# Casts moved off GpSimd, gated weight loads, a table of ranks for 239 tasks, and x block stores in another order

## The chip, the cores and the metric

One core of a Trainium2 chip. The time is the device time of one execution in microseconds (us). A profile's "span" is about 1.7 us shorter than the device time of the same execution. Repeats were taken on five chips, called A to E here, always with the kernel before on the same chip.

## The reference, cut to what matters

```python
q_p, k_p = phi(q), phi(k)                 # phi(x) = max(x, exp(x) - 1 if x <= 0) + 1, 8 x 8 heads, 576 x 64
kv  = einsum('bhsd,bhse->bhde', k_p, v);  z = k_p.sum(2)
att = (q_p @ kv) / (q_p . z)              # -> x, 4608 tokens x 512
P   = exp(x @ w_gate); 8 rounds of row and column normalisation     # 4608 x 8
out = sum_e P[:, e:e+1] * (relu(x @ w1[e]) @ w2[e])                 # 8 experts, 512 -> 1024 -> 512
```

## The kernel before: the parts that the change and the argument touch

The program is a list of tasks with durations, priorities and buffer pools. A small planner places each task on its engine in simulated time; the result is a fixed order for each engine. Attention comes in 16 blocks (numbers 0 to 15), each with one k, q and v input of 576 KB. Expert 0 is computed beside them ("hq" is its first layer, "ye" its second). From about 190 us on, units of the other experts (the sparse part) fill TensorE almost without a gap.

```python
# inputs of block n: blocks 2 and 3 go through GpSimd's queue, behind the first w1 load, the rest through SyncE's
(nc.gpsimd if n in (2, 3) else nc.sync).dma_start(out=..., in_=...)
...
tvv.append(fadd(("pool", 1.3), f_v, deps=[ta, tin["v"]], ...))      # v cast fp32 -> fp16 on GpSimd
vcast[n] = tvv[0]
...
w_t = {0: load_w1(0, prio=-290.0, parts=2, deps=[vcast[0]])}        # weight loads are issued by GpSimd
if b == 1:
    w_t[0] += load_w2(0, prio=-96.5, parts=2, deps=[in_prev[0]])    # w2 of expert 0: behind block 3's inputs
...
w_t[1] = load_w1(1, prio=0.0, after=110.0) + load_w2(1, prio=0.0, after=115.0)
```

The exponential of a k or q block ("ek", "eq") runs on ScalarE. The copy that empties a bank of ye ("acc") runs on ScalarE or VectorE. And each engine works strictly in its order.

The softmax here doesn't subtract the row's maximum and nothing guards it: scores larger than these inputs give would overflow.

## Time and profile before

| | us |
|---|---|
| device time, median of 3 (range) | 982.42 (981.93 to 982.49) |
| the same on chips A to E, medians of 9 to 11 runs | 981.85, 981.97, 981.72, 981.88, 981.87 |
| TensorE busy in the profile | 962.2 of 982.2 |
| device time of the profiled execution | 983.97 |

The profiled execution is 1.5 us slower than the median. And the kernel before has a spread of its own: of its 53 repeats on the five chips, 42 lie at 980.6 to 982.6 and 11 at 983.5 to 985.4.

The view of waits sums, by line, the idle time of an engine and what ended it. For TensorE of the kernel before, from 22.5 to 120 us, the four largest of its ten lines (columns: line, releaser, us in total, times, longest):

```profile
PE hq L536 <- ACT h L540: 2.2, 3, 1.4
PE qt_ps L332 <- DVE tq L281: 1.6, 1, 1.6
PE ye L706 <- DVE acc L223: 0.9, 1, 0.9
PE num_ps L371 <- DVE xn L376: 0.9, 3, 0.4
```

In all ten lines the releaser is VectorE or ScalarE. No line names a DMA: before the change no transfer holds TensorE up directly from 22.5 us on.

### The profile page before, as it was taken

How to read it: one execution, taken by the hardware profiler on the slowest of the kernel's cores; microseconds unless marked ns; L12 is line 12 of the kernel's file. 1: busy time of each engine (PE TensorE's matmuls, PEld its weight loads, DVE VectorE, ACT ScalarE, POOL GpSimd, SP SyncE). 2: the span in 40 equal slices, each digit the busy share in tenths (PEclk: the TensorE clock that was granted, in tenths of full speed). 3: DMA queues.
4: the chain of work that ended last, by engine and by line, in shares of the span. 5: the costliest groups of instructions: out<-in, count | busy, mean ns of one | idle time of the engine just before them, and what ended most of it. 6: DMA issues, size and time to landing. Idle time of an engine off the chain costs nothing.

```text
span 982.2 us, 21403 instructions
## 1 busy us (share of the span) xinstructions
PE 962.2 (98%) x8716; PEld 792.7 (81%) x8716; DVE 771.7 (79%) x1561; ACT 563.2 (57%) x1034; POOL 127.9 (13%) x171
## 2 busy tenths in 40 slices
PE   7899999999999999999999999999999999999997
PEld 4455564488888888888888888888888888888885
DVE  6898869967777777777777777777777777777774
ACT  4798754565555555555555555555555555555552
POOL 4111200001111111111111111111111111111110
PEclk9999999999999999999999999999999999999999
DMA  9886953162226312272225322272225322236663
GB/s 318 257 303 239 265 160 140 65 127 77 75 76 142 97 73 76 76 161 76 77 75 137 101 76 75 76 162 76 76 76 137 102 76 76 76 103 168 161 161 98
DMA packets 47029, 121.99 MB, mean 124 GB/s; under 512 B 4177, under 2 KB 18001, under 8 KB 46929
## 3 DMA queue, kind: packets, MB, share of 16 engines
q1 hardware_dynamic: 32128, 99.76, 30.3%
q0 software_dynamic: 14480, 20.33, 11.5%
q8 instruction: 68, 1.11, 0.5%
q10 hardware_dynamic: 320, 0.52, 0.1%
q14 instruction: 33, 0.26, 0.1%
HBM read 119.69 MB, written 17.69 MB: 140 GB/s over the span
## 4 chain that ended last, share of the span: by engine, by line
PE 89%; DVE 1%; ACT 1%; issue 0%
PE ye L809 33%; PE hq L627 23%; PE att L627 11%; PE Zye L627 6%; PE Zye L809 6%; PE ye L706 5%; PE hq L536 4%; PE xt_ps L387 0%; PE kv_ps L306 0%; PE num_ps L371 0%; PE lg_ps L405 0%; DVE tk L281 0%; PE qt_ps L332 0%; ACT tq L272 0%; PE den_ps L347 0%; ACT qpT L221 0%
## 5 line engine op out<-in xcount | busy, mean ns | idle before, releaser
L823 DVE SCALAR_TENSOR_TENSOR acc<-ye,P_sb,acc 128x256 f32<-128x256 f32 x620 | 264.9, 477 | 95.3 <-PE ye L809 77.9
L627 PEld LDWEIGHTS <-W 128*128 128x128 f16 x2016 | 197.1, 98 | 23.7
L809 PEld LDWEIGHTS <-S 128*128 128x128 f16 x1984 | 194.1, 98 | 22.7 <-issue 0.3
L809 PE MATMUL ye<-T,S 128*128 128x256 f16 x1488 | 192.8, 273 | 0.1
L833 POOL TENSOR_TENSOR acc<-acc,st 128x256 f32<-128x256 f32 x124 | 87.5, 725 | 625.6 <-ACT st L830 620.7
L653 ACT ACTIVATE h<-hq 128x512 f16<-128x512 f32 x126 | 76.3, 606 | 160.8 <-PE hq L627 160.8
L627 PEld LDWEIGHTS <-w 128*128 128x128 f16 x1512 | 147.6, 98 | 23.3 <-issue 1.0
L809 PEld LDWEIGHTS <-h 128*128 128x128 f16 x1488 | 145.6, 98 | 16.8
L627 PE MATMUL hq<-xs,W 128*128 128x256 f16 x1008 | 151.2, 273 | 0.0
L627 PE MATMUL att<-xs,W 128*128 128x256 f16 x1008 | 151.2, 272 | 0.0
L627 PE MATMUL hq<-xs,w 128*128 128x256 f16 x1008 | 140.7, 272 | 0.8 <-DVE h L656 0.8
L782 DVE TENSOR_TENSOR S<-h 128x1024 f16<-128x1024 f16 x124 | 85.4, 688 | 57.9 <-ACT h L653 57.9
L656 DVE CUSTOM_DVE_ANT_0 h<-att,s 128x512 f16<-128x512 f32 x126 | 86.7, 688 | 13.1 <-ACT s L643 13.1
L830 ACT ACTIVATE st<-Zye,P_sb 128x256 f32<-128x256 f32 x124 | 52.1, 471 | 78.0 <-PE Zye L809 78.0
L643 ACT COPY s<-hq 128x512 f32<-128x512 f32 x126 | 75.0, 595 | 36.7 <-PE hq L627 36.7
L650 ACT ACTIVATE h<-Zye 128x512 f16<-128x512 f32 x126 | 75.2, 597 | 35.1 <-PE Zye L627 35.1
L656 DVE CUSTOM_DVE_ANT_0 h<-hq,s 128x512 f16<-128x512 f32 x126 | 86.5, 686 | 0.8 <-PE hq L627 0.7
L639 ACT COPY Zye<-hq 128x512 f32<-128x512 f32 x126 | 73.3, 581 | 16.3 <-PE hq L627 16.3
L706 PE MATMUL ye<-w,h 128*128 128x512 f16 x320 | 77.6, 379 | 0.9 <-DVE acc L223 0.9
L627 PE MATMUL Zye<-xs,w 128*128 128x256 f16 x504 | 75.6, 273 | 0.0
L647 ACT COPY s<-att 128x512 f32<-128x512 f32 x126 | 74.5, 591 | 0.0
L536 PE MATMUL hq<-xT,w 128*128 128x512 f16 x288 | 70.6, 379 | 2.4 <-ACT h L540 2.2
(90 smaller groups left out, 963.1 us busy)
## 6 DMA issues: line engine op xcount, KB each, us to landing
xs<-xd SPq DMA_DIRECT2D x63, 896.0 KB, 4.6
w<-in_moe_w_dram POOLq DMA_DIRECT2D x14, 1024.0 KB, 11.7
out_dram<-acc SPq DMA_DIRECT2D x68, 128.0 KB, 2.4
kin<-in_k_dram SPq DMA_DIRECT2D x14, 576.0 KB, 6.0
qin<-in_q_dram SPq DMA_DIRECT2D x14, 576.0 KB, 5.0
vin<-in_v_dram SPq DMA_DIRECT2D x14, 576.0 KB, 6.4
xd<-xst SPq DMA_DIRECT2D x9, 512.0 KB, 2.6
xd<-xT SPq DMA_DIRECT2D x9, 256.0 KB, 7.1
```

The lines of the kernel that those rows point to most:

```text
L536: nc.tensor.matmul(ghq["tile"], lhsT=gw1["tile"][:, c, ts(f, P)], rhs=xT[:, c, ds(512 * g, 512)], start=(c == 0), stop=(c == NDT - 1))
L627: nc.tensor.matmul(dst[:, p, :], lhsT=lhs(p, c), rhs=rhs(c), start=(first and p == 0 and c == 0), stop=(c == 1), skip_group_check=True)
L643: nc.scalar.copy(out=gs2["tile"], in_=gX["tile"])
L647: nc.scalar.copy(out=gs5["tile"], in_=gR["tile"])
L650: nc.scalar.activation(out=hd(0, 0), in_=Zt[1], func=AF.Relu)
L653: nc.scalar.activation(out=hd(1, 0), in_=gX["tile"], func=AF.Relu)
L656: nc.vector._custom_dve(TENSOR_ADD_SAT, out=dst, in0=ps, in1=sb, s0=3.0e38, s1=0.0)
L706: nc.tensor.matmul(gy[tt]["tile"], lhsT=gh["tile"][:, f, ds(P * tt, P)], rhs=gw2["tile"][:, f, :], start=(f == 0), stop=(f == NFT - 1))
L782: nc.vector.tensor_tensor(out=Sx[:, i], in0=a0, in1=a1, op=op)
L809: nc.tensor.matmul(bank(g_)[:, s, :], lhsT=lhs(s, kk), rhs=rhs(kk), start=(new and s == 0 and kk == 0), stop=(kk == 3), skip_group_check=True)
L823: nc.vector.scalar_tensor_tensor(out=dst(), in0=bank(g_)[:, s, :], scalar=P_sb[:, gg, e:e + 1], in1=dst(), op0=ALU.mult, op1=ALU.add)
L833: nc.gpsimd.tensor_tensor(out=dst(), in0=dst(), in1=gst["tile"], op=ALU.add)
```

## The change

The intent: take the 16 v casts off GpSimd, where they slow VectorE down; issue weight loads when v has landed instead of when its cast is done (a "gate", a copy of four columns); pin 239 tasks to ranks, and 50 of them to one engine too; and put the raw x copies behind the sums. The diff, cut to its core:

```diff
-    p_e = S_.pool(2)
+    p_e = S_.pool(3)                                  # a third buffer of exponentials
-        tvv.append(fadd(("pool", 1.3), f_v, deps=[ta, tin["v"]],
+        tvv.append(fadd(("act", 1.17) if n < 2 else ("dve", 0.75), f_v, deps=[ta, tin["v"]],
-        vcast[n] = tvv[0]
+        if n in (0, 13, 15):
+            def f_gate(_):
+                nc.gpsimd.tensor_copy(out=gate, in_=gin["v"]["tile"][:, 0, 0, 0:4])
+            gates[n] = add(("pool", 0.15), f_gate, deps=[tin["v"]], use=[gin["v"]], prio=pr)
-    w_t = {0: load_w1(0, prio=-290.0, parts=2, deps=[vcast[0]])}
+    w_t = {0: load_w1(0, prio=-290.0, parts=2, deps=[gates[0]])}
+        if g == 0:                                    # the first two hq run in halves
+            jobs = [(f, c, c + 2) for c in (0, 2) for f in range(2)] + jobs[2:]
-        ti = add(("sp", 0.2), f_raw, deps=deps + [t_close], prio=0.0)
+        ti = add(("sp", 0.9), f_raw, deps=deps + [t_close, ti], prio=0.0)   # after the store of the sums
-    w_t[1] = load_w1(1, prio=0.0, after=110.0) + load_w2(1, prio=0.0, after=115.0)
+    w_t[1] = load_w1(1, prio=0.0, deps=[gates[13]]) + load_w2(1, prio=0.0, deps=[gates[15]])
+    ranks = """ 43:-88.9997 46:-94.9994:act 55:-94.9991:dve ... """       # 239 entries, cut here
+    for w in ranks.split():
+        n, p, *en = w.split(":")
+        t = S_.t[int(n)]
+        t["prio"] = float(p)
+        if en:
+            t["eng"] = {en[0]: t["eng"][en[0]]}
```

## The prediction

> **What bounds the kernel now.** I read the page first (busy time by engine and by slice), then the table of windows, then the timelines of TensorE, VectorE and GpSimd in the first 150 us, then the chain of waits.
>
> The table of windows, cut where the behaviour changes (columns: window, length, busy us of PE, weight loads, VectorE, ScalarE and GpSimd with instruction counts, granted clock, DMA share, GB/s):
> ```profile
> 0.00:22.50 22.50, 17.05 (x148) 9.15 (x149) 15.77 (x34) 9.51 (x14) 11.06 (x19) 0.92 0.99 311
> 22.50:120.00 97.50, 88.84 (x963) 53.94 (x961) 85.54 (x178) 83.07 (x132) 19.08 (x16) 1.00 0.85 270
> 120.00:150.00 30.00, 30.00 (x339) 18.38 (x337) 21.21 (x55) 15.51 (x31) 0.00 (x0) 1.00 0.67 183
> 150.00:220.00 70.00, 70.00 (x424) 41.36 (x423) 58.20 (x147) 38.18 (x68) 3.06 (x4) 1.00 0.37 102
> 220.00:975.00 755.00, 754.14 (x6845) 669.04 (x6843) 589.48 (x1147) 416.92 (x792) 94.69 (x132) 1.00 0.35 99
> ```
> From 120 us to 975 us TensorE is never free (at most 0.9 us in 855), at full clock. The chain of waits says the same: 89% of the span is PE. The change touches the attention part, the first expert's first layer and the x block stores, all before about 200 us. So it can only win what TensorE loses in the first 120 us, and the first question is how much that is.
>
> The timeline of TensorE around its first stalls (start, us, engine, what, and in brackets the idle time before it and who ended it):
> ```profile
> 22.53 0.99 PE L536 MATMUL hq<-xT,w 128*128 128x512 f16 x3
> 23.68 1.24 PE L536 MATMUL hq<-xT,w 128*128 128x512 f16 x5 [0.16 <-ACT xT L221]
> 26.29 1.02 PE L536 MATMUL hq<-xT,w 128*128 128x512 f16 x4 [1.36 <-ACT h L540]
> 29.49 0.68 PE L332 MATMUL qt_ps<-ident,tq 128*128 128x128 f16 x9 [1.55 <-DVE tq L281]
> 44.63 1.02 PE L706 MATMUL ye<-w,h 128*128 128x512 f16 x4 [0.95 <-DVE acc L223]
> ```
> The reader sees two regimes. Before 22.53 us TensorE has only the first two attention blocks and 34 filler matmuls on a zero tile. Read from start to start, a 128x512 matmul in a run takes 0.2155 us, and one attention block takes 2.62 us (18 kv 0.63, 9 qt 0.53, 10 den 0.30, 10 num 0.56, 10 xt 0.60). So of 22.53 us, 2 x 2.62 = 5.2 are useful and **17.3 are lost**. After 22.53 us the stalls that the timeline lists up to 120 us are 0.16, 1.36, 1.55, 0.17, 0.95, 0.40, 0.29, 0.77, 0.54, 0.55, 0.27, 0.24, 0.30 and 0.86: **8.4 us**. As a check, counting the work up to 150 us (359 wide matmuls x 0.2155 = 77.4, 16 blocks x 2.62 = 41.9, logits and others 4.4) gives 123.7, so 26.3 are lost, 17.3 + 9.0.
>
> Why those stalls are there shows in the timeline of all engines:
> ```profile
> 6.60 1.43 DVE L281 SCALAR_TENSOR_TENSOR tk<-kin,ek 128x576 f16<-128x576 f32 x2
> 12.39 1.15 POOL L225 CAST vv<-vin 128x1152 f16<-128x1152 f32 x1 [0.28 <-DMA vin<-in_v_dram]
> 12.41 2.40 DVE L281 SCALAR_TENSOR_TENSOR tk<-kin,ek 128x576 f16<-128x576 f32 x2
> 27.06 2.37 DVE L281 SCALAR_TENSOR_TENSOR tq<-qin,eq 128x576 f16<-128x576 f32 x2
> 27.25 1.58 POOL L225 CAST vv<-vin 128x1152 f16<-128x1152 f32 x1 [3.15 <-DMA vin<-in_v_dram]
> ```
> The same pair of VectorE instructions takes 1.43 us alone and 2.37 to 2.40 beside a GpSimd cast. The tq at 27.06 is the one that TensorE waits 1.55 us for at 29.49. The third such case (tk from 41.60, 2.38 us, beside the cast at 41.70) is directly ahead of the acc copy that ends the 0.95 us stall at 44.63.
>
> **What the Trainium skill says.** "SBUF — State Buffer", section "Who interferes with whom": VectorE with two SBUF inputs contends with a GpSimd instruction that reads SBUF, through a port pair the two share. The trace agrees: +0.95 us on a pair, and the cast itself 1.58 instead of 1.15. "VectorE: DVE Perf Modes", section "The perf-mode tier table": a copy from fp32 in SBUF runs at two elements a cycle. No instruction of that form is in the trace, so the cost of the new VectorE cast is an estimate: the fp16 minimum over 1152 elements takes 0.45 us here, at four a cycle and the page's 0.96 GHz 0.30 of that is elements and 0.15 fixed, hence 0.60 + 0.15 = 0.75 us. "Perfetto Trace Analysis", section "Identifying the Most-Contended Engine": matmul busy time is a poor measure since matmuls overlap. The trace agrees (a wide matmul is listed with 379 ns on average and costs 215), so I count start to start.
>
> **The change part by part.**
> (1) *No cast on GpSimd.* Removed: 16 casts x 1.238 = 19.8 us of an engine that is idle anyway. Removed with them: the collisions, from the group means against the clean times tk 22 x (0.923 - 0.715) = 4.6, tq 16 x (0.814 - 0.715) = 1.6, ek 16 x (0.550 - 0.450) = 1.6, eq 16 x (0.496 - 0.450) = 0.7, together 8.5 us of VectorE. Added: 14 x 0.75 = 10.5 us on VectorE, 2 x 1.17 = 2.3 on ScalarE (taken as its exp on the same shape, 1.166). Pinned ranks move other work: up to the last xT copy VectorE does 1 acc copy for 6, 24 kvz copies for 30 and 14 xT copies for 16; ScalarE 19, 40 and 18 for 10, 34 and 16. Counts by group means: VectorE 121.9 to 118.1 us, ScalarE 112.3 to 122.8 (parts of neighbours overlap, so true occupancy is lower). Neither fills the 137 us that this stretch takes.
> (2) *Gated weight load.* The first load is issued when a 4-column copy ends, not a 1.15 us cast: about 8.0 us for 9.00. DMA is saturated from there to 40 us (share 1.09 to 1.14 in ten-microsecond windows), so what follows lands about 1 us earlier.
> (3) *Order at the start.* I walked the new order by hand with durations of the trace. The first blocks' tq is made by ScalarE add plus VectorE maximum, the second block's tk comes uncollided at 13.0 (14.8 before), its xn ends at 21.4 (22.1), xT at 22.8 (23.6). Two hq matmuls run ahead of the last transposes; 16 are done by 26.1, with one wait of about 1 us for the relu to free a bank; the v cast of the third block ends at 27.2 and its kv matmuls at 27.8. Before, the same work (16 hq, kv, qt) was done at 30.9: 3.1 ahead. At 33.0 the new order has 32 hq and two blocks' kv done; before had 28 hq at 35.46, and needs 0.86 more: **3.3 us** gained.
> (4) *Stalls after 42 us*: 5.2 of the 8.4. Those behind VectorE lateness should shrink, but the new order is just as fixed, and a few late results must be expected. I take 2.2 as left: **3.0 us** gained.
> (5) *Stores.* Before, the raw copies went out at 104 to 139 us, now each follows its own sums, from about 140 to 180. The x tile's memory is reused from 195 us, when the last hq of the first expert is read. The sums end at 179.8, a transfer lands in 7 us: 187, hidden. **0.**
> Sum: 982.4 - 3.3 - 3.0 = **976.1**.
>
> **Rivals.** *The start is bound by DMA*: third and fourth v landed at 22.95 and 27.25, and reordering does not move bytes. Then part 3 gives 1 and the total is 978.5. For it: share above 1.0. Against it: 1.36 and 1.55 us of stalls there are ended by ScalarE and VectorE. *ScalarE becomes the bound*: 10.5 us more on it, and every hq bank waits for its relu. New waits of hq on h would eat parts 3 and 4: 981 to 984. Against it: it is idle 13 of the first 22.5 us. *The ranks fit the chip well*: almost all stalls vanish, 17.3 - 1 and about 1 left: 973. *The late stores hold up the x tile's release or the first xs load*: some us lost near 195 to 210; I see 8 us of slack.
>
> **Range and chances.** All that can be won is about 8.4 to 9 plus 1 to 1.5 at the start, so 972 is the floor, and 2% (962.8) is out of reach. Repeats lie within 0.6 us. The ScalarE rival alone sets the upper end, at half its effect: range 972.8 to 980.2. Faster by over 2%: 1%, within 2%: 98%, slower: 1%.
>
> **What would show it.** Right: no VectorE tk or tq pair above 1.6 us; v casts of 0.75 on VectorE; first hq near 21 and ye near 33; stalls after 22 us summing to 3 or 4; the windows from 220 us unchanged. Wrong: hq waiting on h again and again (ScalarE), waits on DMA at kv, idle TensorE between 180 and 215 (stores), or casts of 1.3 us on VectorE.

## The result, and the profile after

| | median us | runs |
|---|---|---|
| after | 980.35 | 977.64, 980.62, 981.61, 980.07 |
| before, same chip | 982.17 | 981.43 to 982.49 (4 runs) |

The ratio is 0.9979, 95% interval 0.9957 to 1.0001. A ratio is the mean time of one kernel's fast runs over that of the other's fast runs of the same rounds, so not quite the ratio of the medians. The class is "same", as predicted, but 980.35 lies just outside the range. The runs are as telling as the median: 4 us apart, where the prediction reckoned with 0.6.

The profiled run after is the fastest of the four (977.64). Its table of windows, the answer to the one of before:

```profile
0.00:22.50 22.50, 16.98 (x153) 9.31 (x154) 14.47 (x36) 14.08 (x18) 9.32 (x18) 1.00 0.98 311
22.50:120.00 97.50, 93.71 (x985) 55.85 (x984) 84.52 (x179) 89.18 (x152) 2.00 (x4) 1.00 0.84 259
150.00:220.00 70.00, 70.00 (x452) 44.06 (x451) 62.15 (x156) 37.38 (x67) 7.27 (x6) 1.00 0.61 175
```

TensorE is busy 93.71 of the 97.5 us in the front against 88.84 before. GpSimd falls from 19.08 to 2.00 us, and between 150 and 220 us TensorE is never idle, as before. The timeline of TensorE:

```profile
20.48 0.59 PE L545 MATMUL hq<-xT,w 128*128 128x512 f16 x2
25.84 0.68 PE L335 MATMUL qt_ps<-ident,tq 128*128 128x128 f16 x9 [0.33 <-DVE tq L281]
32.68 1.03 PE L718 MATMUL ye<-w,h 128*128 128x512 f16 x4
36.98 1.02 PE L718 MATMUL ye<-w,h 128*128 128x512 f16 x4 [1.36 <-DMA w<-in_moe_w_dram]
108.66 1.02 PE L718 MATMUL ye<-w,h 128*128 128x512 f16 x4 [0.52 <-ACT acc L221]
```

The first hq comes at 20.48 us (22.53 before), the first ye at 32.68 (35.58), and the wait for tq is 0.33 (1.55). Then come two waits that the kernel before does not have: **1.36 us for a weight tile** and **0.52 us for a bank copy**. On VectorE (timeline) the pair beside which a cast used to run is back at its clean time, and the new cast costs what was estimated:

```profile
11.31 1.43 DVE L281 SCALAR_TENSOR_TENSOR tk<-kin,ek 128x576 f16<-128x576 f32 x2
24.36 1.43 DVE L281 SCALAR_TENSOR_TENSOR tq<-qin,eq 128x576 f16<-128x576 f32 x2
25.70 0.76 DVE L223 CAST vv<-vin 128x1152 f16<-128x1152 f32 x1
```

The chain that ended last shows where the two new waits come from. In order of time (start, us, what) it now holds, after one q input at the start, two transfers:

```profile
17.95 18.99 DMA w<-in_moe_w_dram
97.76 9.05 DMA kin<-in_k_dram
```

The first is the second half of expert 0's w2. It is issued when it always was (17.2 us for the pair, 17.5 before), but takes 19.0 us to land. The view of transfers has the two halves together, with the median from issue to landing; first the kernel before, then the changed one:

```profile
w<-in_moe_w_dram POOLq DMA_DIRECT2D x2, 512.0 KB, 13.8
```
```profile
w<-in_moe_w_dram POOLq DMA_DIRECT2D x2, 512.0 KB, 16.5
```

SyncE now issues block 4's k at 24.02 instead of 26.72, since the buffers come free earlier, and ye asks for the tile 2.9 us earlier. The second is the last k input (block 15). One microsecond behind its issue, at 98.91, GpSimd issues the second expert's w1 (1 MB as it lands; the 2 MB in some expectations counts it as read, in fp32), released by the gate on block 13's v; before, that load left at 112.35, behind all inputs. On ScalarE's timeline the k input is what the next three steps hang on:

```profile
106.83 1.16 ACT L266 ACTIVATE ek<-kin 128x1152 f16<-128x1152 f32 x1 [0.77 <-DMA kin<-in_k_dram]
108.02 0.58 ACT L221 COPY acc<-ye 128x512 f32<-128x512 f32 x1
```

The exponential waits for k, the bank copy stands behind the exponential, and TensorE waits for the bank (0.52 us at 108.66).

### The profile page after: what moved, and what is told of

Same layout as the page of the kernel before. It is cut to its first block, busy times and chain, and to the rows that moved or that the text cites. A ratio compares the mean times of both kernels' runs of the same rounds, so it can differ in the third digit from the quotient of the medians.

```text
span 975.9 us, 21395 instructions
## 1 busy us (share of the span) xinstructions
PE 960.9 (98%) x8716; PEld 791.7 (81%) x8716; DVE 767.9 (79%) x1562; ACT 568.9 (58%) x1049; POOL 111.9 (11%) x158
## 4 chain that ended last, share of the span: by engine, by line
PE 91%; DMA 3%; ACT 3%; DVE 1%; issue 1%; POOL 0%; SPq 0%; DVEq 0%; ACTq 0%; POOLq 0%
PE ye L821 33%; PE hq L639 23%; PE att L639 11%; PE ye L718 6%; PE Zye L639 6%; PE Zye L821 6%; PE hq L545 4%; DMA w<-in_moe_w_dram 2%; DMA kin<-in_k_dram 1%; ACT eq L266 1%; PE xt_ps L390 1%; ACT h L549 1%; DMA qin<-in_q_dram 1%; PE num_ps L374 0%; ACT tq L272 0%
## 5 line engine op out<-in xcount | busy, mean ns | idle before, releaser
L821 PEld LDWEIGHTS <-S 128*128 128x128 f16 x1984 | 194.1, 98 | 22.5
L651 ACT COPY Zye<-hq 128x512 f32<-128x512 f32 x126 | 73.2, 581 | 17.5 <-PE hq L639 17.5
```

The costliest lines, as they stand in the source:

```text
L821: nc.tensor.matmul(bank(g_)[:, s, :], lhsT=lhs(s, kk), rhs=rhs(kk), start=(new and s == 0 and kk == 0), stop=(kk == 3), skip_group_check=True)
```

## The experiments

The theory: the order of the changed kernel has little slack, so two transfers that share the DMA engines with others (w2 at 37 us, the last k at 107 us) turn into waits, of a length that varies from run to run. The main rivals: the granted clock of the run makes the spread; the late stores cost; the ranks or the casts do not bring what was reckoned.

### The changed kernel again, three times (chip A)

No edit.

> The changed kernel itself, five rounds. Four runs so far gave 977.64 to 981.61, the kernel before 981.43 to 982.49. Theory D (the front now hangs on DMA landings: the w2 half load took 19.0 us in the one trace and a kin load 9.05 us, both on the chain of waits): the spread of 3 to 4 us comes back, with every span 974 to 980 and the kernel before again within 1 us. Theory C (the clock gate: some runs have TensorE at half clock for a few us in the front): the spread comes back too, but the slow runs are those with the lower mean clock (0.995 against 1.0), in order. Theory N (it was noise of one chip): spread under 1.5 us, median near 977 or near 981.

> A second trace of the changed kernel. Theory D: if this execution is slower than 977.6, TensorE's stalls that are longer than in the first trace (1.8 us of lost time at 36.98 behind w2) are behind a DMA landing, and the windows from 220 us on are the same. Theory C: the window table shows a granted clock under 1.00 in the front and the matmuls there at 427 ns start to start.

> A third trace of the changed kernel, same expectations as the second: theory D a longer stall behind w2 or an input load, theory C a window with clock under 1.00 after 20 us.

Measured: again 979.42 median (976.46 to 979.90, and one run of 985.61), ratio 0.9978 (0.9952 to 1.0003). The two looks gave 981.68 and 976.93. Their traces differ mainly in the two waits and the clock after one of them. The slower one, timeline of ScalarE and TensorE:

```profile
109.07 1.16 ACT L266 ACTIVATE ek<-kin 128x1152 f16<-128x1152 f32 x1 [2.71 <-DMA kin<-in_k_dram]
110.90 1.36 PE L718 MATMUL ye<-w,h 128*128 128x512 f16 x4 [2.65 <-ACT acc L221]
```

and its windows (columns as above; the third number from the end is the granted clock):

```profile
110.00:112.00 2.00, 1.10 (x4) 0.44 (x4) 0.00 (x0) 1.98 (x4) 0.00 (x0) 0.86 1.05 355
112.00:114.00 2.00, 2.00 (x13) 1.40 (x12) 0.74 (x2) 1.52 (x3) 0.00 (x0) 0.50 0.38 149
114.00:116.00 2.00, 2.00 (x35) 1.06 (x34) 1.74 (x3) 0.93 (x4) 1.22 (x2) 0.78 0.00 0
```

After a stall of 2.65 us the clock falls to half for some microseconds, which costs another 2 x (0.14 + 0.50 + 0.22) = 1.7 us. In the faster look the same exponential starts at 105.94 without a wait, and w2 holds TensorE up for 0.65 us. The mean clock of a run does not order the runs: both looks have 0.998, since the faster one's dip lies at 8 to 14 us and costs little there: its first hq comes at 21.00 us, against 20.62 in the slower look. So the clock follows a stall here and lengthens it; it is not what starts the spread.

### The stores alone undone (chip A)

```diff
-        ti = add(("sp", 0.9), f_raw, deps=deps + [t_close, ti], prio=0.0)
+        ti = add(("sp", 0.9), f_raw, deps=deps + [t_close], prio=0.0)
```

> One part undone: the raw x copies no longer wait for the sums in issue order. My working: 0 us, equal to the changed kernel within its spread (976 to 981). If the stores' order was worth something (rival): 2 us or more either way, and the windows between 140 and 220 us show idle TensorE in the slower of the two.

Measured: 980.92 (977.69 to 981.18), ratio 0.9978, as the changed kernel beside it. Inconclusive at this size: its profile has the part from the first sparse unit to the end at 788.2 us (979.0 - 190.79) against 787.0 (975.9 - 188.86), with some 0.7 us of TensorE's idle time at 190 to 220 us, but that is one trace. The edit is also not the stores alone: the planner put 76 of VectorE's and 18 of TensorE's instructions in other places, from about 145 us on, so the stores' own worth stays unsettled.

### One cause away at a time (chip B)

The second expert's w1 issued with its w2; nothing else in any engine's order moves (the traces have the same order of instructions, apart from this issue):

```diff
+                if e == 1 and nm == "w1":       # held, and issued ahead of the next weight load
+                    held.append(go)
+                    return
```

> The changed kernel with one issue moved: the second expert's w1 load (2 MB) leaves right ahead of its w2 load, at about 114 us, in place of 98.9 us; the order of every instruction on TensorE, VectorE, ScalarE and SyncE is that of the changed kernel. Theory (the early load shares the DMA engines with the last k block, whose exponential stands ahead of a bank copy on ScalarE): the k load of the last block lands 6 to 7.5 us after its issue in place of 8.0 to 11.2, ScalarE does not wait for it, TensorE has no stall over 0.4 us between 104 and 112 us, the granted clock does not dip there, and the fast runs lie at 975.5 to 977.5 within 2 us of each other. Rival (the spread has another cause, the clock of the chip or the rest of the kernel): the stall goes but the fast runs still spread over 3 us, with a median of 979 to 980.5. Second rival (the weights now come too late): TensorE waits for w1 of the second expert after 120 us, and the time is 980 or more.

Block 4's inputs through GpSimd's queue, so behind w2; the orders of TensorE, VectorE and ScalarE stay, as the traces show:

```diff
-                (nc.gpsimd if n in (2, 3) else nc.sync).dma_start(
+                (nc.gpsimd if n in (2, 3, 4) else nc.sync).dma_start(
```

> The changed kernel with the inputs of block 4 issued from GpSimd's queue behind the first expert's w2 load in place of SyncE's, so that the second half of w2 shares the DMA engines with less; all other orders stay. Theory: the second half of w2, 18.99 us from issue to landing in the changed kernel, takes 17 us or less, the 1.36 us stall of TensorE at 37 us falls under 0.5, and the time falls by 0.8 to 1.3 us; the run-to-run spread of 3 us stays, as the early w1 load is still there: median 978 to 979.5. Rival (the transfer is bound by bytes and not by who is ahead): the wait moves to block 4's own inputs, and the time stays at 979 to 980.5.

> Both edits of the two runs beside it. Theory: the two gains add: no stall over 0.5 us at 37 us nor between 104 and 112 us, fast runs at 974.5 to 976.5 within 2 us of each other, 0.6 to 0.8 per cent under the kernel before and clear of it. Rival (one of them has another cause): no better than the better of the two alone, 977 or more, or a spread of 3 us.

The early w1 put into the kernel before. This edit is not as clean: from 107 us on the planner gave ScalarE, VectorE and TensorE another order, so it shows a new plan with an early w1:

```diff
-    w_t[1] = load_w1(1, prio=0.0, after=110.0) + load_w2(1, prio=0.0, after=115.0)
+    w_t[1] = load_w1(1, prio=0.0, deps=[vcast[13]]) + load_w2(1, prio=0.0, after=115.0)
```

> The kernel before with one line of the change alone: the second expert's w1 load held only to the v cast of block 13, not behind all inputs. Theory (the early load delays the last k block and hurts a schedule whose ScalarE has little slack there): the last k block lands 8 us or more after its issue in place of 6.2 to 7.3, and TensorE's stalls between 100 and 115 us grow by 0.5 to 2.5 us: 982.5 to 984.5, with a wider spread. Rival (only the tighter order of the changed kernel has no slack): the k block lands later, but the time stays within 0.5 us of the kernel before, 981.5 to 982.5.

| chip B | median us | runs | ratio (95%) |
|---|---|---|---|
| w1 held | 979.00 | 977.92 to 982.10 | 0.9967 (0.9949 to 0.9984) |
| block 4 behind w2 | 975.87 | 975.71 to 975.92, and one of 977.83 | 0.9935 (0.9919 to 0.9950) |
| both | 975.80 | 975.56 to 976.26 | 0.9931 (0.9916 to 0.9945) |
| before with early w1 | 981.42 | 981.21 to 981.88 | 0.9988 (0.9972 to 1.0005) |

The two halves of w2 land in 12.7 us (block 4 behind w2) and 13.8 us (both edits) in the median, near the 13.8 of the kernel before, and in 17.8 with w1 held alone. The view of transfers with block 4 behind w2:

```profile
w<-in_moe_w_dram POOLq DMA_DIRECT2D x2, 512.0 KB, 12.7
```

This landing varies by itself, too: in the kernel before with early w1, whose order is that of the kernel before up to that time, the median is 15.4.

Three of my expectations missed. With w1 held the wait at 108 us was gone, as expected, but the spread was not: in its profile the wait for w2 is 2.66 us, and the clock falls behind it (0.95 and 0.71 in the two five-microsecond windows from 35 us). And block 4's inputs behind w2 came out 3.1 us under w1 held alone, and 3.5 to 4.5 under the changed kernel's medians on other chips (it did not run on chip B), where 0.8 to 1.3 was expected, with little spread; that left open whether the early w1 mattered at all, or whether chip B was kind. The kernel before with early w1 loses nothing (981.42 against 981.97), where 0.5 to 2.5 us were expected, although its last k then takes 12.3 us to land: the exponential of that k starts only 13.7 us after the issue (112.72 against 99.04), so it does not wait. In the kernel before it starts 7.4 us after the issue (108.72 against 101.28), which 12.3 would have held up. So it is the new order that hides the landing, and what the early w1 alone would cost is not shown. The view of transfers, issue to landing of that one k input, for the kernel before with early w1:

```profile
kin<-in_k_dram SPq DMA_DIRECT2D x1, 576.0 KB, 12.3
```

### The parts of the change by themselves (chip C)

> The changed kernel itself once more, on the chip of the three runs beside it (it was not among those of the earlier set with block 4 on GpSimd's queue). Theory (its loss is two waits on DMA landings, for the second half of the first expert's w2 at 37 us and for the last k block at 107 us, each of a length that changes from run to run): fast runs between 976.4 and 982 and more than 2 us apart, with a median 2 to 4 us over the 975.9 of block 4 on GpSimd's queue. Rival (that result belongs to its chip): this kernel lies at 976 to 977 here as well, all runs within 1 us.

> Block 4's inputs on GpSimd's queue, the table of ranks kept, and the v casts back on GpSimd (the ranks were searched without them, and five engine choices of ScalarE casts fall out). Theory (casts on GpSimd cost through slowed VectorE instructions, 1.3 us of lateness each where they meet): VectorE's pair instructions that run beside a cast take up to 1.4 us in place of 0.75, and the time is 978.5 to 981, 2.6 to 5 us over the same kernel with the casts on VectorE. Rival (the ranks are the gain, and the cast is worth nothing by itself): within 1 us of 975.9.

> Block 4's inputs on GpSimd's queue and the casts off GpSimd, but without the table of ranks, so that the plan's own order stands. Theory (the table is what brings hq, kv and ye forward; its removal costs what the prediction gave it and more): first hq later than 21.5 us, more TensorE stalls between 22 and 120 us (5 us or more in all), and 978.5 to 981.5. Rival (the table adds little once the casts are gone): 975.5 to 977.

> Block 4's inputs on GpSimd's queue, casts on GpSimd and no ranks: what is left of the change are the third buffer of exponentials, the split first hq, the gates and the order of the stores. Theory (the two parts do not stand alone, casts and ranks make the gain): 981 to 984, the level of the kernel before. Rival (gates, buffer and split carry it): 977 to 979.

The edits, on top of block 4 behind w2, each alone and both:

```diff
-        tvv.append(fadd(("act", 1.17) if n < 2 else ("dve", 0.75), f_v, deps=[ta, tin["v"]],
+        tvv.append(fadd(("pool", 1.3), f_v, deps=[ta, tin["v"]],
-    for w in ranks.split():
+    for w in []:
```

| chip C | median us | runs |
|---|---|---|
| after, unchanged | 981.67 | 977.73 to 983.83 |
| block 4 behind w2, casts on GpSimd | 1007.69 | 1007.41 to 1009.61 |
| block 4 behind w2, no ranks | 980.47 | 980.00 to 981.00 |
| block 4 behind w2, casts on GpSimd, no ranks | 989.45 | 987.20 to 989.87 |

The changed kernel shows its worst here, at the level of the kernel before. Its profiled run (983.83) waits twice for w2, timeline of TensorE and the windows after it:

```profile
34.39 1.02 PE L718 MATMUL ye<-w,h 128*128 128x512 f16 x4 [1.27 <-DMA w<-in_moe_w_dram]
40.00 1.86 PE L718 MATMUL ye<-w,h 128*128 128x512 f16 x4 [2.68 <-DMA w<-in_moe_w_dram]
```
```profile
35.00:40.00 5.00, 2.32 (x31) 1.57 (x29) 0.88 (x3) 3.33 (x4) 0.00 (x0) 0.91 1.12 361
40.00:45.00 5.00, 5.00 (x18) 2.28 (x18) 1.89 (x3) 0.65 (x3) 0.00 (x0) 0.50 0.51 168
45.00:50.00 5.00, 5.00 (x53) 2.95 (x52) 3.60 (x8) 3.61 (x6) 0.00 (x0) 0.90 0.01 3
```

The two waits are 3.95 us together, and the clock lost 5 x (0.09 + 0.50 + 0.10) = 3.45 us: 7.4 us from one transfer. The expectation had its runs at 976.4 to 982, so it was too narrow.

Without ranks, and without the wait for w2, the time is 980.47 and tight, 4.6 us over the same kernel with ranks on chip B, and 2.4 to 3.5 over its later medians on chips D and E. Both expectations with casts on GpSimd (978.5 to 981 and 981 to 984) missed by far. The two kernels with casts on GpSimd do not tell the price of the casts: block 4's inputs and the casts then stand in one queue and hold each other up, and the first of them also has 15.1 us of waits on VectorE's accumulations after 200 us that no kernel with the casts on VectorE shows. That is why the casts were undone once more without the block 4 edit.

### One part undone in the changed kernel itself, and the pair on one chip (chip D)

> The changed kernel, beside block 4 on GpSimd's queue on one chip. Theory (waits for the second half of w2 and for the last k block, each of a length that changes from run to run, the longest followed by a fall of the granted clock): fast runs 976.5 to 984, over 2 us apart. Rival (those runs were of another chip): 975.5 to 976.5 within 0.5 us.

> The changed kernel with block 4's inputs behind the w2 load on GpSimd's queue, on the chip of the run of the changed kernel beside it. Theory: most runs at 975.5 to 976.5 here too, 1 to 6 us under the changed kernel's of the same chip; no wait of TensorE for a weight tile. Rival (chance or chip): median over 978, or as spread as the changed kernel.

> The changed kernel with the v casts back on GpSimd and all else kept, block 4's inputs on SyncE as well (in the earlier run with casts on GpSimd block 4's inputs queued behind a cast on that engine, and the later part held 15 us of waits that no other run shows, so that it did not tell the cast's own price). Theory (the casts cost 4 to 8 us in the front through VectorE instructions stretched beside a cast and through inputs and weights that queue behind casts): the first unit of the sparse part starts at 193 to 197 us in place of 188.9, tk pairs beside a cast take up to 1.4 us. Rival (it was only block 4's place in the queue): starts at 188 to 191.

> The changed kernel without the table of ranks. Theory (the table is worth 4.6 us where w2 does not wait, as the run with block 4 on GpSimd's queue showed; with the wait it is worth less, as the forward moved bank copies and ye only reach that wait sooner): 980.5 to 984, with a wait for w2 of 1 us or more. Rival (without the table ye comes so late that no wait for w2 is left): 980 to 981 within 1 us, as with block 4 on GpSimd.

| chip D | median us | runs |
|---|---|---|
| after, unchanged | 979.42 | 977.55 to 984.12 |
| block 4 behind w2 | 978.10 | 976.53 to 979.81 |
| casts on GpSimd | 1006.04 | 1004.75 to 1008.06 |
| no ranks | 983.03 | 982.45 to 983.34 |

Block 4 behind w2 was not tight here, and the expected 975.5 to 976.5 for most runs missed: two of five lie at 976.5 and 976.6, the others at 978.1 and over. The little spread on chip B had been luck. Its profile has no wait for a weight tile, but the other one in full, timeline of ScalarE and TensorE:

```profile
107.28 1.16 ACT L266 ACTIVATE ek<-kin 128x1152 f16<-128x1152 f32 x1 [2.72 <-DMA kin<-in_k_dram]
109.10 1.25 PE L718 MATMUL ye<-w,h 128*128 128x512 f16 x4 [2.47 <-ACT acc L221]
```

So the two waits are separate, and each has its own cause. Without ranks the wait for w2 is there too (0.95 and 2.66 us, with no fall of the clock after it; its four runs agree within 0.9 us, so such a wait need not vary), and the kernel is 1.1 us over the one before on that chip, which is not clear of noise (ratio 1.0010, 0.9997 to 1.0024). By medians the ranks are worth 983.03 - 979.42 = 3.6 us here, though one run of the changed kernel (984.12) is slower than all without ranks.

With the casts on GpSimd the first sparse unit starts at 193.28 us, within the 193 to 197 expected; in the run of both edits on chip E below it starts at 186.86. The waits that TensorE's timeline lists from 22.5 to 130 us sum to 7.3 us against 1.6 in that run. But the reason I gave does not carry it: the tk pairs have a mean of 795 ns against 755, and a single pair is stretched, to 2.24 us at 71.13. The rest is order, and 15.1 us of waits on VectorE's accumulations stand in the sparse part again:

```profile
PE ye L821 <- DVE acc L835: 15.1, 2, 9.9
```

The traces show why, which I had overlooked. The sums into the experts' outputs (acc, with P as a factor) need the end of the normalisation rounds on VectorE. In the changed kernel the last logits matmuls run at 138.5 us and the rounds end at 180.9. With the casts on GpSimd and the ranks kept, the last logits come at 176.4 and the rounds end at 216.6 (220.3 with block 4 behind w2), and the waits follow. Without the table they end at 190.0, so it is the table on a plan that it was not made for. Of the 26.6 us over the changed kernel's median, 24.4 lie after the first sparse unit (1004.7 - 193.28 = 811.4 us against 787.0), 15.1 of them in these waits. The price of the casts alone stays open.

### Both causes away against one (chip E)

> The changed kernel with block 4's inputs behind the w2 load and the second expert's w1 load held to the issue of its w2 load, on the chip of the run beside it. Theory (both waits on DMA landings, one at 37 us and one at 107 to 109 us, have then lost their cause): fast runs at 975.5 to 976.5 and within 1 us of each other on this chip too, no stall of TensorE over 0.5 us between 30 and 120 us, granted clock 1.00 from 20 us on. Rival (a chip of that day sets the spread): 977 or more in half of the runs.

> The changed kernel with block 4's inputs behind the w2 load only. Theory (the wait for the last k block stays where the w1 load leaves one microsecond behind it, and comes in some runs): at least one run in five 1 us or more over the fastest, and a median at or over that of the kernel beside it, 975.8 to 978.5. Rival (the early w1 load costs nothing): equal to the kernel beside it within 0.3 us, run for run.

| chip E | median us | runs | ratio (95%) |
|---|---|---|---|
| both | 975.77 | 975.46 to 976.43 | 0.9933 (0.9920 to 0.9945) |
| block 4 behind w2 | 976.93 | 975.98 to 978.73 | 0.9945 (0.9930 to 0.9961) |

This is the answer of the pair: with w1 held as well the runs lie within 1 us of each other, and with the early w1 within 2.8. The medians are 1.2 us apart here and 0.1 on chip B, and the intervals overlap, so the size of this second cause rests on the traces. In its profile the one with early w1 has a wait of 1.01 us behind the last k, the one with both edits none. TensorE's waits over 0.15 us from 22.5 to 120 us with both edits, by the view of waits, in full:

```profile
PE hq L554 <- ACT h L558: 0.7, 3, 0.3
PE den_ps L359 <- ACT kvz L229: 0.4, 1, 0.4
PE qt_ps L344 <- DVE tq L290: 0.3, 1, 0.3
PE kv_ps L318 <- DVE vv L231: 0.2, 1, 0.2
```

No DMA and no acc is left. (Line numbers are 9 higher from the added lines.) The view of transfers for the last k input, first the changed kernel, then both edits:

```profile
kin<-in_k_dram SPq DMA_DIRECT2D x1, 576.0 KB, 9.0
```
```profile
kin<-in_k_dram SPq DMA_DIRECT2D x1, 576.0 KB, 7.0
```

The version with both edits beats both kernels: 0.67 to 0.69% under the one before on two chips, where the change as it stands has 0.1 to 0.2% with intervals that reach over 1.

## Why the prediction was wrong, and where it was right

**The accounting.** For each trace of the changed order, take from the span the wait for w2, the wait behind the last k, and the clock lost after them (length of a window times one minus its granted clock):

| trace | last k lands in | w2 wait | k wait | clock | span | rest |
|---|---|---|---|---|---|---|
| look 3, chip A | 8.0 | 0.65 | 0 | 0 | 975.1 | 974.5 |
| after, first result | 9.0 | 1.36 | 0.52 | 0 | 975.9 | 974.0 |
| again, chip A | 9.3 | 1.37 | 0.78 | 0 | 976.5 | 974.3 |
| look 2, chip A | 11.2 | 1.32 | 2.65 | 1.7 | 979.9 | 974.2 |
| after, chip C | 9.2 | 3.95 | 0.65 | 3.45 | 982.0 | 974.0 |
| after, chip D | 8.8 | 2.79 | 0.29 | 1.7 | 978.9 | 974.1 |
| w1 held, chip B | 7.4 | 2.66 | 0 | 1.7 | 978.4 | 974.0 |
| block 4 behind w2, chip B | 8.1 | 0 | 0 | 0 | 974.1 | 974.1 |
| block 4 behind w2, chip E | 9.6 | 0 | 1.01 | 0 | 974.8 | 973.8 |
| block 4 behind w2, chip D | 11.0 | 0 | 2.47 | 1.7 | 978.0 | 973.8 |
| both, chip B | 7.4 | 0 | 0 | 0 | 974.1 | 974.1 |
| both, chip E | 7.0 | 0 | 0 | 0 | 974.0 | 974.0 |

Spans from 974.0 to 982.0 fall together to 973.8 to 974.5. So three quantities explain the spread of these traces to within 0.7 us. Left out is the kernel with the old order of the stores, whose later part has another order; there 2 us stay unexplained (a start 0.6 us later, and about 1.1 in the part after 190 us). The slowest runs of the changed kernel (985.61, 984.12) left no trace.

Now the steps, in the prediction's order.

- **What bounds the kernel, and the floor**: right. All that moved lies before 190 us; from the first sparse unit on, the profiled runs before and after take the same 787 us (982.2 - 194.99 = 787.2, 975.9 - 188.86 = 787.0).
- **Part 1, the casts**: the VectorE cast was estimated at 0.75 us and measured 0.747; no pair over 1.43 us is left. The collisions were counted with 0.715 us for one clean instruction; the changed kernel's mean for tk and tq is 0.755 (two of a pair overlap), which makes them about 7.1 us and not 8.5. What their end is worth by itself could not be separated, but one pair of traces gives a hint. Up to 97 us the trace of the kernel before with early w1 has the very order of the kernel before. There v of block 3 lands 0.65 us later, so its cast misses the tq (timelines of VectorE and TensorE):

```profile
26.77 1.43 DVE L281 SCALAR_TENSOR_TENSOR tq<-qin,eq 128x576 f16<-128x576 f32 x2
28.26 0.68 PE L332 MATMUL qt_ps<-ident,tq 128*128 128x128 f16 x9 [0.67 <-DVE tq L281]
```

TensorE waits 0.67 us in place of 1.55, and the 0.95 us at 44.63 is missing too, as no cast meets that tk. So these collisions cost the slower trace 1.8 us, and whether they happen is a matter of landings in the kernel before as well.
- **Part 2, the gated loads: here, and in part 3, is the step that failed: transfers were taken as fixed or only earlier.** Part 2 costed one gate of three, the first, and only as a gain: "what follows lands about 1 us earlier". (That load left at 8.45 us, for the expected 8.0 and 9.00 before.) The gate on block 13 moved a 1 MB load 13 us forward, to one microsecond behind the last k. With w1 early that k took 8.0 to 11.2 us to land in the profiled runs, with it held 7.0 to 7.4, and 6.2 in the kernel before. TensorE waited 0 to 2.65 us for it.
- **Part 3, the start**: right in size, with 3.3 us reckoned. The first ye came at 32.68 for "near 33", the third block's kv matmuls at 26.51 for 27.2. But it took the transfers as fixed, and that is the larger half of what failed: TensorE waited 0.65 to 3.95 us for w2. Being early cuts the time w2 has until it is needed by 2.9 us and sends block 4's inputs out 2.7 us earlier, beside w2, whose halves then land in 15.8 to 19.2 us in the median. The prediction named "waits on DMA" as a sign of being wrong, yet looked for them at kv, not at ye.
- **Part 4, "I take 2.2 as left"**: that was after 42 us, and for waits on engines it was too much: 0.8 were left of 5.2 (1.6 in all after 22.5 us). The waits on transfers had no term at all: 1.9 us in the first profile, up to 4.6 in a later one, with up to 3.45 of clock after them.
- **Part 5, the stores**: 0 reckoned, unsettled.
- **The rivals**: "the start is bound by DMA" was the nearest, at 978.5 (its own terms give 978.4, and those of "the ranks fit" about 974, not 973), but for another reason: not v that lands late, but w2. ScalarE as the bound did not come: hq waits for its relu 0.7 us in all in the first profile, 1.2 at most in the others of that order. It came in through the back door, as the engine whose fixed order hands one late k on to a bank of TensorE.
- **The range**: "repeats lie within 0.6 us" was taken from three runs of the kernel before. It holds neither for the changed kernel nor, over more runs, for the kernel before.

**The sum fits the kernel without the two waits, in part by luck.** Reckoned were 3.3 + 3.0 = 6.3 us; with both causes away the gain is 981.87 - 975.77 = 6.1, at 975.8 for the predicted 976.1. But the losses were read in an execution of 983.97 us and taken off a median of 982.4. From that trace to the one of both edits the front shrinks by 194.99 - 186.86 = 8.1 us, of which 4.3 are the waits after 42 us (3.0 reckoned) and 3.8 the start (3.3). So the gains were reckoned too small by 1.8, and the base was too low by 1.5. Of the gain, the changed kernel gives some 4 back in the median of the first result (980.35 - 975.8 = 4.5); its one traced run shows 1.9 of waits on the two transfers, and the later traces show up to 8. The three slower runs of that result were not traced.

What stays open: the price of the casts alone, the stores, the third buffer of exponentials and the split first hq (never undone by themselves), and why a landing takes 8 us in one run and 11 in the next with the same issues around it. SyncE's own issue of that k does not tell: it takes 0.96 us at the 11.2 landing, but 0.73 at one of 7.4, and 0.39 at both 8.0 and 9.2.

## What to carry to other kernels

When an order gets tighter, re-time the transfers as well as the compute: every buffer that frees earlier sends a transfer earlier, beside one that is now needed earlier. A load that is not needed for 80 us should not, where there is a choice, leave a microsecond behind one that is needed in 8, even if the queue is free. If repeats of a kernel begin to spread, compare two traces of it wait by wait before suspecting the chip, and see whether the trace that you read is of a usual run: the difference may be one transfer, made larger by the clock that falls after a long stall.

## What the Trainium skill lacked or had wrong

- "TensorE: Matmul & The Clock Gate", section "Part 1: The HAM clock gate", says that the clock falls to half after an idle window of about 3.4 us, and that the window runs freely. Here shorter stalls were enough: 2.47 us (down to 0.50), 2.65 and 2.68 (0.50), 2.66 (0.71 over five us), 2.79 (0.76), and 1.80 among other stalls in the run with block 4 behind w2, casts on GpSimd and no ranks (0.76). Without ranks a stall of 2.66 us had no fall after it, nor had 1.81 with casts on GpSimd. Ahead of the first kv matmuls, at 7 to 10 us, a stall of 1.67 us has a fall behind it (block 4 behind w2, no ranks: 0.57 from 10 to 14 us) and one of 3.09 has none (after, chip C). That about the same length does both fits a free-running window; the length that the page gives is not what these runs show as needed.
- "DMA: Bandwidth & Descriptors", section "Queues, rings and completion order", says that a DMA engine takes turns between the queues that have work. The runs fit this, though they show only that the two share: a 1 MB load on GpSimd's queue, issued 1.0 to 1.6 us after a 576 KB input on SyncE's, takes that input from 7.0 to 7.4 us to 8.0 to 11.2. No page that I read gives a size for how much such a landing varies from run to run; here it is 3 us.
- "VectorE: DVE Perf Modes", section "The perf-mode tier table": nothing to mend; the cast estimated from it at 0.75 us took 0.747.
